# Splitting weights and activations in a fused attention, MoE and gated-MoE kernel: fewer weight operations per block, and every low part of the two MoE layers subtracted on VectorE

## The chip, the cores and the metric

One core of one Trainium2 chip runs the whole kernel. The metric is the device time of one execution in microseconds. Before the change the median of three runs is 702.15 us (702.01 to 702.81).

## The reference, cut to what matters

Three layers in float32, one behind the other: attention with pairs of queries averaged, a feed-forward layer with ELU, and a gated layer behind an RMS norm.

```
attn: q_pool = q.reshape(B, H, S//2, 2, D).mean(axis=3)        # 2, 8, 1152, 64
      softmax(q_pool @ k.T / sqrt(D)) @ v                      -> x: 1152 x 512
moe:  h = x @ w_in ; g = where(h > 0, h, exp(min(h, 0)) - 1)   # w_in 512 x 2048
      x = g @ w_out                                            # 2048 x 512
moe2: xn = x / sqrt(mean(x*x) + 1e-6) * rms_g
      (silu(xn @ w_gate) * (xn @ w_val)) @ w_out               # 512 x 1536, 1536 x 512
```

## The kernel before, in words

All activations lie transposed: 128 features on the partitions, 1152 tokens in three column blocks c of 384 tokens. TensorE multiplies a product in three passes: each operand a is split into a high part (a rounded copy, made on ScalarE) and a low part (a minus its high part), and `product` (L162) issues high by high (L167), high weight by low activation (L168) and low weight by high activation (L169) for each of four slices of 128 features. So a **product** is 12 matmuls of 128 by 384 into one of eight PSUM banks, which `bank` (L535) hands out in turn.

The order of the work on each engine is the order in which the program is written; every engine works through its own list in that order, and waits there for others.

**The weights** come as 64-bit numbers and are made into float32 by a generator, `Stream.work` (L97), 68 blocks of 128 x 512 in the order of use (in this text W0 to W67). One call of `next` on it, one *weight operation*, emits one of nine steps: the absolute value on ScalarE (L113), the low word on VectorE (L115), then the tail of the block before it, which is a step that allocates its two buffers, the high part on ScalarE (L141) and the low part (L143), and then four more steps on VectorE (L120, L122, L124, L128). `ws.step(i, k)` (L148) advances it by k, unless it is eight blocks ahead of block i. `ws.get(i)` hands out a block. Three blocks, W0 to W2, are made during the attention.

**The first MoE layer** runs in two halves of 1024 hidden features (loop L590). In each half, eight blocks i of 128 hidden features are computed for three column blocks c: one product, then `elu` (L180): ScalarE takes relu and exp (L183, L184), VectorE combines them with the bank (L187), and one product later, in `flush`, ScalarE makes the high part `gh` (L188) and GpSimd the low part `gl`. Around it stand two `ws.step(wi, 2)`. Then `out1` (L602) multiplies back: for each block m of 128 output features a quad q of four blocks, for three c. In the second half the sum is added on VectorE (L607) and squared on ScalarE (L561); GpSimd adds the squares of m = 1 and 2 (L563), VectorE those of m = 3.

The last two m of the second half are written the other way round, **the column loop** (L621): for each c, the four products n = 0 to 3 (m = 2 and 3, two quads each). Behind n = 1 of column block c, `norms[c - 1].sums` sums the squares on TensorE (L568) and takes the root (L571) and reciprocal (L572); behind n = 2, `norms[c - 1].scale` spreads it with transposes (L578) and, for four m, rescales x on VectorE (L581), makes `xh` on ScalarE (L583) and `xl`, in turn on GpSimd (even m) and on VectorE (odd m). The sums and the rescaling of the third column block stand behind the first products of the second MoE layer.

**The second MoE layer**: `unit(i, c)` (L645) is two products (gate W(32 + 2i), value W(33 + 2i)), `swiglu` (L636) takes silu on ScalarE (L638), multiplies on VectorE (L641), and one unit later makes `uh` and `ul`. The units (0, 0) and (0, 1) are multiplied first; then stands the rescaling of the third column block; then the two `swiglu` of these units, and then the units (1, 0), (1, 1), (0, 2), (1, 2) and so on.

Low parts go through two helpers: `lo_pool` (L62, recorded as line L63) on GpSimd and `lo_dve` (L68, line L69) on VectorE.

Of the kernel before, what the change touches and what calls it, by code (L numbers as in the profile page):

```python
# [38 lines left out]
def tile_kernel(ctx: ExitStack, tc: tile.TileContext, qd, kd, vd, w1d, w2d, wgd, wvd, wod, rgd, outd):  # L39
# [33 lines left out]
    class Stream:  # L73
# [60 lines left out]
        def split(self, i, w):  # L134
            self.at, self.alloc = i, True
            yield
            self.alloc = False
            pool, n = self.pools[i % WB >= NE]
            h, l = (pool.tile([128, 4, 128], F32R, tag=f"w{a}", name=f"w{a}", bufs=n) for a in "hl")
            h2, l2 = (a.rearrange("p k c -> p (k c)") for a in (h, l))  # L140
            T.copy(h2, w)  # L141
            yield
            lo_pool(l2, w, h2)  # L143
            self.parts[i] = (h, l)
            self.done += 1
            yield
# [30 lines left out]
        while pending:  # L177
            pending.pop(0)()

    def elu(ps, gh, gl, lo):  # L180

        e = hp.tile([128, CH], F32, tag="e", name="e", bufs=4)
        T.activation(out=e, in_=ps, func=AF.Relu, scale=-1.0)  # L183
        T.activation(out=e, in_=e, func=AF.Exp, scale=-1.0)  # L184
        flush()
        ws.step(wi, 2)
        V.scalar_tensor_tensor(out=e, in0=e, scalar=-1.0, in1=ps, op0=ALU.add, op1=ALU.max)  # L187
        pending.append(lambda: (T.copy(gh, e), lo(gl, e, gh)))  # L188
        ws.step(wi, 2)

    w_in = [w1d[i] for i in range(16)]
    w_out = [w2d[i] for i in range(16)]
# [326 lines left out]
    early(1)  # L519
    early(2)  # L520
    for n in range(NE):
        elu(fb[:, n, 0:CH], ge[0][:, n, :], ge[1][:, n, :], lo_pool)
    actx.close()


# [24 lines left out]
    class Norm:  # L550
# [5 lines left out]
        def square(self, m):  # L556
            c = self.c
            if m == 0:
                self.s = cp.tile([128, CH], F32, tag="sq", name="sq", bufs=3)
            q = self.s if m == 0 else hp.tile([128, CH], F32, tag="e", name="sqm", bufs=4)  # L560
            T.activation(out=q, in_=x2[:, m, cs(c)], func=AF.Square)  # L561
            if m:
                (V if m == 3 else G).tensor_tensor(out=self.s, in0=self.s, in1=q, op=ALU.add)  # L563

        def sums(self):
            b = bank()
# [7 lines left out]
        def scale(self):  # L574
            b = bank()
            c = self.c
            for n in range(3):
                PE.transpose(b[:, 128 * n:128 * n + 128], self.r[:, n:n + 1].to_broadcast([128, 128]), ident)  # L578
            for m in range(4):
                x = x2[:, m, cs(c)]  # L580
                V.scalar_tensor_tensor(out=x, in0=x, scalar=rg[:, m:m + 1], in1=b, op0=ALU.mult, op1=ALU.mult)  # L581
                h, l = xh[:, m, cs(c)], xl[:, m, cs(c)]
                T.copy(h, x)  # L583
                (lo_dve if m % 2 else lo_pool)(l, x, h)

    norms = [Norm(c) for c in range(3)]

# [2 lines left out]
    for hf in range(2):  # L590
        for i in range(8):
            w = ws.get(wi)
            for c in range(3):
                if hf == 0 and c == 0 and i < NE:
                    continue
                ps = bank()
                product(ps, w, xchunk(c), True, True)
                elu(ps, gh[:, i, cs(c)], gl[:, i, cs(c)], lo_dve if c == 1 and hf else lo_pool)
            wi += 1
        flush()  # L600

        def out1(c, m, q, b, w):  # L602
            product(b, w, g_quad(hf, q, c), q == 0, q == 1)
            if q == 1:
                x = x2[:, m, cs(c)]
                if hf:
                    V.tensor_tensor(out=x, in0=b, in1=x, op=ALU.add)  # L607
                    norms[c].square(m)
                else:
                    T.copy(x, b)  # L610

        for m in range(2 if hf else 4):
            bs = [bank() for c in range(3)]
            for q in range(2):
                for c in range(3):
                    out1(c, m, q, bs[c], ws.get(wi + q))
                    ws.step(wi + q, 4)
            wi += 2
        if hf:
            T.activation(out=dummy, in_=eps, func=AF.Sqrt)  # L620
            for c in range(3):  # L621
                for n in range(4):
                    m, q = 2 + n // 2, n % 2
                    if q == 0:
                        b = bank()
                    out1(c, m, q, b, ws.get(wi + n))
                    if c < 2 or n < 2:
                        ws.step(wi + (n if c == 2 else 0), 3)
                    if c and n == 1:
                        norms[c - 1].sums()  # L630
                    if c and n == 2:
                        norms[c - 1].scale()
            wi += 4


    def swiglu(i, c, pg, pv):  # L636
        s = hp.tile([128, CH], F32, tag="e", name="sl", bufs=4)
        T.activation(out=s, in_=pg, func=AF.Silu)  # L638
        flush()
        ws.step(wi + 2 * i if i > 1 else wi, 4)  # L640
        V.tensor_tensor(out=s, in0=pv, in1=s, op=ALU.mult)  # L641
        h, l = uh[:, i, cs(c)], ul[:, i, cs(c)]
        pending.append(lambda: (T.copy(h, s), (lo_dve if c == 1 else lo_pool)(l, s, h)))

    def unit(i, c, between=None):  # L645
        b = bank(), bank()
# [90 lines left out]
```

## Time and profile before

| | |
|---|---|
| median of three runs | 702.15 us |
| the profiled execution's own time | 702.12 us |
| its span in the profile | 700.3 us |
| TensorE matmul busy | 681.4 us (97%) |
| VectorE busy | 543.8 us (78%) |
| ScalarE busy | 416.0 us (59%) |
| GpSimd busy | 377.6 us (54%) |
| low parts of weights on GpSimd | 68 of 1467 ns |
| low parts of ELU's result on GpSimd | 37 of 1214 ns, and 3 of 1018 ns |
| low parts of the gated product on GpSimd | 24 of 1090 ns |

The attention takes the first 262 us or so, the first half of the first MoE layer lasts to about 365 us, the second to about 476 us, and the second MoE layer to the end. Time is read on TensorE: where it is idle or at a lower clock, the kernel loses time; where another engine is idle, it loses none by that alone. The page's engine rows give averages over these stages, so the table above doesn't tell which engine is late where.

### The profile page before, as it was taken

Reading aid. Unit: us, or ns where it says so; the run is one execution under the profiler, and the core shown is the slowest. Engines: PE = TensorE matmul, PEld = TensorE weight load, DVE = VectorE, ACT = ScalarE, POOL = GpSimd, SP = SyncE. Lnnn points to the kernel's source line nnn. Section 1 sums busy time; section 2 is a strip of 40 time slices with the busy share of each in tenths; the row PEclk is TensorE's granted clock in tenths of the full one; section 3 lists DMA queues with packets and bytes.
Section 4 is the critical chain, followed back from the end, with each engine's and each line's share of the span. In section 5 each row is a group of like instructions: output and inputs, shape, how many; then the busy total and the mean of one; then the engine's idle time right before and its main releaser. Section 6 shows DMA issues by size and latency. Waiting matters only on the chain.

```text
span 700.3 us, 11344 instructions
## 1 busy us (share of the span) xinstructions
PE 681.4 (97%) x4243; PEld 668.9 (96%) x4243; DVE 543.8 (78%) x891; ACT 416.0 (59%) x855; POOL 377.6 (54%) x332
## 2 busy tenths in 40 slices
PE   7999999999999999997999999999999999999998
PEld 6999999989898999986999999999999999999997
DVE  6888889898989967999978999756999876585000
ACT  5888889889887957675447774434454444342000
POOL 5988789887988305665434545442454443342000
PEclk9999999999999999997999999999999999999999
DMA  5423323433432001223432222200323222222000
GB/s 181 141 85 123 115 87 101 146 116 110 142 102 65 1 31 43 80 90 99 147 129 78 66 87 91 90 1 31 121 91 107 104 91 91 90 95 91 35 35 34
DMA packets 21607, 62.34 MB, mean 89 GB/s; under 512 B 2736, under 2 KB 4784, under 8 KB 21552
## 3 DMA queue, kind: packets, MB, share of 16 engines
q1 hardware_dynamic: 21552, 61.62, 26.6%
q8 instruction: 33, 0.54, 0.3%
q14 instruction: 22, 0.18, 0.1%
HBM read 59.25 MB, written 2.36 MB: 88 GB/s over the span
## 4 chain that ended last, share of the span: by engine, by line
PE 82%; DVE 11%; ACT 3%; POOL 1%; issue 1%; DVEq 0%; ACTq 0%; POOLq 0%
PE b L167 17%; PE b L168 17%; PE b L169 17%; PE s L279 10%; PE o L323 9%; PE t L297 8%; DVE p L283 2%; DVE ptl L69 2%; DVE wt L124 2%; DVE wt L122 2%; DVE wt L120 1%; DVE e L187 1%; POOL wl L63 1%; DVE wt L128 1%; POOL gl L63 1%
## 5 line engine op out<-in xcount | busy, mean ns | idle before, releaser
L167 PE MATMUL b<-xh,wh 128*128 128x384 f32 x468 | 157.4, 336 | 0.5 <-ACT sl L638 0.5
L169 PE MATMUL b<-xh,wl 128*128 128x384 f32 x468 | 157.1, 336 | 0.0
L168 PE MATMUL b<-xl,wh 128*128 128x384 f32 x468 | 157.0, 335 | 0.0
L63 POOL TENSOR_TENSOR wl<-wt,wh 128x512 fp32r<-128x512 f32 x68 | 99.7, 1467 | 73.9 <-ACT wh L141 57.0
L283 DVE TENSOR_SCALAR_CACHE_REDUCE p<-s 128x1152 f32<-128x1152 f32 x72 | 97.3, 1352 | 21.1 <-PE s L279 20.2
L69 DVE TENSOR_TENSOR ptl<-t,pth 128x384 fp32r<-128x384 f32 x216 | 106.6, 548 | 2.7 <-ACT pth L305 2.1
L279 PE MATMUL s<-kd,qt 128*128 128x384 f32 x480 | 97.7, 341 | 6.5 <-DVE p L283 5.0
L305 ACT CAST pth<-t 128x384 fp32r<-128x384 f32 x216 | 89.2, 487 | 23.3 <-PE t L297 22.7
L288 ACT ACTIVATE p<-p,st 128x1152 f32<-128x1152 f32 x72 | 91.3, 1268 | 6.5 <-DVE p L283 6.2
L279 PEld LDWEIGHTS s<-kd,qt 128*128 128x128 f32 x480 | 81.3, 188 | 9.7 <-DVE p L283 3.4
L167 PEld LDWEIGHTS b<-xh,wh 128*128 128x128 f32 x468 | 87.9, 188 | 1.1 <-ACT sl L638 0.9
L168 PEld LDWEIGHTS b<-xl,wh 128*128 128x128 f32 x468 | 88.0, 188 | 0.0
L169 PEld LDWEIGHTS b<-xh,wl 128*128 128x128 f32 x468 | 87.9, 188 | 0.0
L297 PE MATMUL t<-ident,p 128*128 128x128 f32 x648 | 85.7, 275 | 0.0
L113 ACT ACTIVATE wt<-wr 128x512 f32<-128x512 f32 x68 | 46.0, 676 | 66.3 <-POOL wl L63 50.3
L323 PE MATMUL o<-pth,vd 128*128 128x256 f32 (+1 forms) x288 | 84.4, 315 | 0.0
L124 DVE SCALAR_TENSOR_TENSOR wt<-wr,wt 128x512 uint32<-128x512 uint32 x68 | 80.2, 1179 | 1.8
L297 PEld LDWEIGHTS t<-ident,p 128*128 128x128 f32 x648 | 73.9, 141 | 6.6 <-DVE ptl L69 4.3
L323 PE MATMUL o<-ptl,vd 128*128 128x256 f32 (+1 forms) x288 | 78.5, 295 | 0.0
L63 POOL TENSOR_TENSOR gl<-e,gh 128x384 fp32r<-128x384 f32 x37 | 44.9, 1214 | 45.7 <-ACT gh L188 45.7
L167 PE MATMUL b<-gh,wh 128*128 128x384 f32 x180 | 62.4, 346 | 5.2 <-ACT gh L188 4.6
L128 DVE CUSTOM_DVE_ANT_0 wt<-wt,we 128x1024 uint16<-128x1024 uint16 x68 | 65.8, 968 | 1.9
(113 smaller groups left out, 1320.5 us busy)
## 6 DMA issues: line engine op xcount, KB each, us to landing
wr<-in_w_dram SPq DMA_DIRECT2D x32, 512.0 KB, 3.2
rawk<-in_k_dram SPq DMA_DIRECT2D x32, 288.0 KB, 2.9
rawq<-in_q_dram SPq DMA_DIRECT2D x15, 576.0 KB, 4.0
wr<-in_wg_dram SPq DMA_DIRECT2D x12, 512.0 KB, 3.2
wr<-in_wv_dram SPq DMA_DIRECT2D x12, 512.0 KB, 3.2
wr<-in_wo_dram SPq DMA_DIRECT2D x12, 512.0 KB, 3.2
rawv<-in_v_dram SPq DMA_DIRECT2D x16, 288.0 KB, 2.8
out_dram<-o SPq DMA_DIRECT2D x12, 192.0 KB, 1.8
```

The costliest lines, as they stand in the source:

```text
L63: G.tensor_tensor(out=o, in0=i, in1=f(h), op=ALU.subtract)
L69: V.tensor_tensor(out=o, in0=i, in1=f(h), op=ALU.subtract)
L124: V.scalar_tensor_tensor(out=t, in0=hi, scalar=0x80000000, in1=t, op0=ALU.bitwise_and, op1=ALU.bitwise_xor)
L167: PE.matmul(out, lhsT=wh[:, k, :], rhs=ah, start=first and k == 0, stop=False)
L168: PE.matmul(out, lhsT=wh[:, k, :], rhs=al, start=False, stop=False)
L169: PE.matmul(out, lhsT=wl[:, k, :], rhs=ah, start=False, stop=last and k == 3)
L279: PE.matmul(s[:, m, 0:384], lhsT=a, rhs=b[:, 384 * m:384 * m + 384], start=n == 0, stop=n == len(parts) - 1)
L283: V.tensor_scalar(out=pt, in0=s[:, :, 0:384], scalar1=-0.0625, scalar2=None, op0=ALU.mult, op1=ALU.min, accum_out=st[p][:, 0, TILES[i][4], :])
L288: T.activation(out=pt, in_=pt, func=AF.Exp, scale=-1.0, bias=st[p][:, 0, TILES[i][4], :], accum_out=st[p][:, 1, TILES[i][4], :])
L297: PE.transpose(ps[:, k, :], src[:, 128 * b:128 * b + 128], ident)
L305: T.copy(oh, re(ps))
L323: PE.matmul(self.o[:, 0:self.N], lhsT=v[:, b, :], rhs=(pth, ptl)[u][:, g["buf"], b, g["c0"]:320], start=self.n == 0, stop=self.n == 17)
```

## The change

Five places put low parts on VectorE that were on GpSimd: the weights', ELU's, the gated product's, and the norm's (`xl` of even m); the two sums of squares that GpSimd added go there too. So GpSimd has nothing to do behind the attention. The weight operations around each ELU go from 2 + 2 to 1 + 2 in the first half (nine for a block's three column blocks) and to 1 + 1 in the second (six).

```diff
@@ split
-            lo_pool(l2, w, h2)
+            lo_dve(l2, w, h2)
@@ elu
-    def elu(ps, gh, gl, lo):
+    def elu(ps, gh, gl, k=2):
...
         flush()
-        ws.step(wi, 2)
+        ws.step(wi, 1)
         V.scalar_tensor_tensor(out=e, in0=e, scalar=-1.0, in1=ps, op0=ALU.add, op1=ALU.max)
-        pending.append(lambda: (T.copy(gh, e), lo(gl, e, gh)))
-        ws.step(wi, 2)
+        pending.append(lambda: (T.copy(gh, e), lo_dve(gl, e, gh)))
+        ws.step(wi, k)
@@ the three products before the loop
-        elu(fb[:, n, 0:CH], ge[0][:, n, :], ge[1][:, n, :], lo_pool)
+        elu(fb[:, n, 0:CH], ge[0][:, n, :], ge[1][:, n, :])
@@ Norm.square
-                (V if m == 3 else G).tensor_tensor(out=self.s, in0=self.s, in1=q, op=ALU.add)
+                V.tensor_tensor(out=self.s, in0=self.s, in1=q, op=ALU.add)
@@ Norm.scale
-                (lo_dve if m % 2 else lo_pool)(l, x, h)
+                lo_dve(l, x, h)
@@ the first MoE layer
-                elu(ps, gh[:, i, cs(c)], gl[:, i, cs(c)], lo_dve if c == 1 and hf else lo_pool)
+                elu(ps, gh[:, i, cs(c)], gl[:, i, cs(c)], 2 - hf)
@@ swiglu
-        pending.append(lambda: (T.copy(h, s), (lo_dve if c == 1 else lo_pool)(l, s, h)))
+        pending.append(lambda: (T.copy(h, s), lo_dve(l, s, h)))
```

TensorE's list is the same before and after but for the buffers that it names. Three places on the other engines follow (the numbers behind names are buffers).

VectorE in the first half, in the middle of the blocks (L187 combines ELU, `wt`, `we` and `wr` are a weight being made); before:

```order
L187 SCALAR_TENSOR_TENSOR e_3569<-e_3569,b_3556 128x384
L115 TENSOR_SCALAR we_3579<-wr_3310 128x512
L187 SCALAR_TENSOR_TENSOR e_3596<-e_3596,b_3583 128x384
L120 TENSOR_SCALAR wt_3580<-wt_3580 128x512
L122 TENSOR_SCALAR wt_3580<-wt_3580 128x512
L124 SCALAR_TENSOR_TENSOR wt_3580<-wr_3310,wt_3580 128x512
L187 SCALAR_TENSOR_TENSOR e_3620<-e_3620,b_3607 128x384
L128 ISA wt_3580<-wt_3580,we_3579 128x1024
```

The same place now, one round of three ELUs:

```order
L187 SCALAR_TENSOR_TENSOR e_3592<-e_3592,b_3579 128x384
L115 TENSOR_SCALAR we_3597<-wr_3310 128x512
L69 TENSOR_TENSOR gl_3530<-e_3592,gh_3529 128x384
L187 SCALAR_TENSOR_TENSOR e_3615<-e_3615,b_3602 128x384
L69 TENSOR_TENSOR wl_3621<-wt_3496,wh_3620 128x512
L120 TENSOR_SCALAR wt_3598<-wt_3598 128x512
L69 TENSOR_TENSOR gl_3530<-e_3615,gh_3529 128x384
L122 TENSOR_SCALAR wt_3598<-wt_3598 128x512
L187 SCALAR_TENSOR_TENSOR e_3639<-e_3639,b_3626 128x384
L124 SCALAR_TENSOR_TENSOR wt_3598<-wr_3310,wt_3598 128x512
L128 ISA wt_3598<-wt_3598,we_3597 128x1024
L69 TENSOR_TENSOR gl_3530<-e_3639,gh_3529 128x384
```

Three `gl` and one `wl` have come in for every three ELUs, and there is one weight for three ELUs where there were four for nine.

VectorE in the column loop, about the first rescaling (L607 adds to x, L563 adds a square, L572 is the reciprocal, L581 rescales); before:

```order
L607 TENSOR_TENSOR x2_3525<-b_5362,x2_3525 128x384
L563 TENSOR_TENSOR sq_5161<-sq_5161,sqm_5392 128x384
L607 TENSOR_TENSOR x2_3525<-b_5395,x2_3525 128x384
L572 RECIPROCAL rr_5428<-rr_5428 128x3
L581 SCALAR_TENSOR_TENSOR x2_3525<-x2_3525,rg_61,b_5444 128x384 x2
L69 TENSOR_TENSOR xl_69<-x2_3525,xh_68 128x384
...
L607 TENSOR_TENSOR x2_3525<-b_5431,x2_3525 128x384
L563 TENSOR_TENSOR sq_5182<-sq_5182,sqm_5473 128x384
```

Now:

```order
L607 TENSOR_TENSOR x2_3525<-b_5349,x2_3525 128x384
L563 TENSOR_TENSOR sq_5119<-sq_5119,sqm_5379 128x384
L69 TENSOR_TENSOR wl_5383<-wt_5307,wh_5382 128x512
L120 TENSOR_SCALAR wt_5363<-wt_5363 128x512
L572 RECIPROCAL rr_5391<-rr_5391 128x3
L122 TENSOR_SCALAR wt_5363<-wt_5363 128x512
L124 SCALAR_TENSOR_TENSOR wt_5363<-wr_5287,wt_5363 128x512
L128 ISA wt_5363<-wt_5363,we_5362 128x1024
L581 SCALAR_TENSOR_TENSOR x2_3525<-x2_3525,rg_61,b_5412 128x384
L69 TENSOR_TENSOR xl_69<-x2_3525,xh_68 128x384
L581 SCALAR_TENSOR_TENSOR x2_3525<-x2_3525,rg_61,b_5412 128x384
```

A weight's operations stand between the square, the reciprocal and the rescaling, and each rescaling is followed by its own `xl`.

ScalarE at the third rescaling, where the second MoE layer begins (L583 makes `xh`, L638 is silu, L113 and L141 are a weight's); before:

```order
L583 CAST xh_68<-x2_3525 128x384 x4
L638 ACTIVATE sl_5646<-b_5563 128x384
L113 ACTIVATE wt_5654<-wr_5359 128x512
L638 ACTIVATE sl_5658<-b_5589 128x384
L643 CAST uh_5644<-sl_5646 128x384
L141 CAST wh_5662<-wt_5376 128x512
```

Now:

```order
L583 CAST xh_68<-x2_3525 128x384 x4
L638 ACTIVATE sl_5623<-b_5540 128x384
L113 ACTIVATE wt_5626<-wr_5409 128x512
L141 CAST wh_5629<-wt_5445 128x512
L638 ACTIVATE sl_5634<-b_5566 128x384
L643 CAST uh_5621<-sl_5623 128x384
```

And TensorE now, in unit (1, 0): the end of its first product and the start of its second:

```order
L168 MATMUL b_5648<-xl_69,wh_5461 128x384
L169 MATMUL b_5648<-xh_68,wl_5462 128x384
L167 MATMUL b_5649<-xh_68,wh_5629 128x384
L168 MATMUL b_5649<-xl_69,wh_5629 128x384
L169 MATMUL b_5649<-xh_68,wl_5630 128x384
```

The second product of unit (1, 0) reads W35, whose high part `wh_5629` now stands on ScalarE behind the four `xh` of the third rescaling; before, that product read `wh_5336`, which stood ahead of the first rescaling.

## Rows read from the trace of the kernel before

**Rows 1.** The page's first part: busy time, share of the span and instructions of TensorE (matmuls, weight loads) and the other engines.

```profile
PE 681.4 (97%) x4243; PEld 668.9 (96%) x4243; DVE 543.8 (78%) x891; ACT 416.0 (59%) x855; POOL 377.6 (54%) x332
```

**Rows 2.** What TensorE waited for in the MoE layers: us in total, times, longest.

```profile
PE b L167 <- ACT gh L188: 4.6, 1, 4.6
PE b L168 <- POOL gl L63: 1.1, 1, 1.1
PE b L568 <- DVE sq L563: 0.8, 1, 0.8
PE b L167 <- DVE e L187: 0.6, 1, 0.6
PE b L167 <- ACT sl L638: 0.5, 1, 0.5
```

**Rows 3.** Stretches of the span: start:end, length, busy time (and instructions) of PE, PEld, DVE, ACT, POOL, then TensorE's granted clock as a share of 2.4 GHz, the DMA share and GB/s.

```profile
316.00:317.00 1.00, 0.00 (x0) 0.00 (x0) 1.00 (x4) 0.27 (x1) 0.00 (x0) 0.87 0.95 311
...
326.00:328.00 2.00, 2.00 (x11) 2.00 (x10) 1.97 (x3) 0.37 (x1) 0.81 (x1) 0.75 0.00 0
```

**Rows 4.** TensorE in order of time, about the wait in the first half: start, duration, engine, line, operation, tiles, shapes, and in brackets the idle time before it and what ended it. A matmul starts before the one ahead of it has ended.

```profile
314.23 0.33 PE L169 MATMUL b<-gh,wl 128*128 128x384 f32 x1
319.16 0.69 PE L167 MATMUL b<-gh,wh 128*128 128x384 f32 x1 [4.59 <-ACT gh L188]
```

**Rows 5.** The chain that ended last, in the stretch behind that wait: start, share of the chain, what. Between the first two rows shown lie 15 more of 0.32 us.

```profile
321.60 0.32 PE b L169
...
326.72 0.32 PE b L167
327.04 0.22 PE b L168
327.26 0.18 PE b L169
```

**Rows 6.** VectorE in order of time in the first half (columns as in rows 4). From the first to the last row shown lie nine ELUs (L187) and four weights.

```profile
282.70 1.03 DVE L124 SCALAR_TENSOR_TENSOR wt<-wr,wt 128x512 uint32<-128x512 uint32 x1
...
305.49 1.40 DVE L122 TENSOR_SCALAR wt<-wt 128x512 uint32<-128x512 uint32 x1
...
307.27 1.05 DVE L124 SCALAR_TENSOR_TENSOR wt<-wr,wt 128x512 uint32<-128x512 uint32 x1
```

**Rows 7.** GpSimd in order of time, the subtraction beside that L122.

```profile
305.13 1.48 POOL L63 TENSOR_TENSOR wl<-wt,wh 128x512 fp32r<-128x512 f32 x1
```

**Rows 8.** VectorE in order of time in the second MoE layer, where GpSimd was idle beside these.

```profile
606.16 0.43 DVE L122 TENSOR_SCALAR wt<-wt 128x512 uint32<-128x512 uint32 x1
606.62 0.69 DVE L124 SCALAR_TENSOR_TENSOR wt<-wr,wt 128x512 uint32<-128x512 uint32 x1
607.69 0.56 DVE L69 TENSOR_TENSOR ul<-sl,uh 128x384 fp32r<-128x384 f32 x1 [0.38 <-ACT uh L643]
608.16 0.68 DVE L128 CUSTOM_DVE_ANT_0 wt<-wt,we 128x1024 uint16<-128x1024 uint16 x1
608.77 0.42 DVE L115 TENSOR_SCALAR we<-wr 128x512 f32<-128x512 uint32 x1
609.10 0.55 DVE L641 TENSOR_TENSOR sl<-b,sl 128x384 f32<-128x384 f32 x1
```

**Rows 9.** VectorE in order of time during the attention: the reduction of the scores (L283) behind the place where W0's low part now stands, the step L120 of a weight beside a GpSimd subtraction, and the same step by itself.

```profile
172.38 1.34 DVE L283 TENSOR_SCALAR_CACHE_REDUCE p<-s 128x1152 f32<-128x1152 f32 x1
...
175.05 1.51 DVE L120 TENSOR_SCALAR wt<-wt 128x512 f32<-128x512 f32 x1
...
206.66 0.41 DVE L120 TENSOR_SCALAR wt<-wt 128x512 f32<-128x512 f32 x1
```

**Rows 10.** VectorE in order of time about the rescalings (an L581 row of x2 is two of them).

```profile
453.89 0.56 DVE L607 TENSOR_TENSOR x<-b,x 128x384 f32<-128x384 f32 x1 [2.29 <-PE b L169]
...
456.97 1.14 DVE L581 SCALAR_TENSOR_TENSOR x<-x,rg,b 128x384 f32<-128x384 f32 x2 [1.61 <-PE b L578]
...
462.14 0.54 DVE L607 TENSOR_TENSOR x<-b,x 128x384 f32<-128x384 f32 x1
463.35 0.56 DVE L563 TENSOR_TENSOR sq<-sq,sqm 128x384 f32<-128x384 f32 x1 [0.66 <-ACT sqm L561]
...
478.78 1.14 DVE L581 SCALAR_TENSOR_TENSOR x<-x,rg,b 128x384 f32<-128x384 f32 x2 [2.04 <-PE b L578]
480.51 0.95 DVE L69 TENSOR_TENSOR xl<-x,xh 128x384 fp32r<-128x384 f32 x1 [0.58 <-ACT xh L583]
```

**Rows 11.** ScalarE in order of time behind the third rescaling: two `xh`, a silu, and the two ScalarE steps of a weight.

```profile
479.43 1.04 ACT L583 CAST xh<-x 128x384 fp32r<-128x384 f32 x2 [1.39 <-DVE x L581]
...
482.96 0.48 ACT L638 ACTIVATE sl<-b 128x384 f32<-128x384 f32 x1
483.34 0.66 ACT L113 ACTIVATE wt<-wr 128x512 f32<-128x512 f32 x1
...
486.79 0.61 ACT L141 CAST wh<-wt 128x512 fp32r<-128x512 f32 x1
```

**Rows 12.** TensorE in order of time about the norm: the sums of the second column block, the transposes of the third, and the first product of unit (1, 1).

```profile
463.96 0.83 PE L568 MATMUL b<-ones,sq 128*128 128x1 f32 x6 [0.76 <-DVE sq L563]
...
478.26 0.49 PE L578 MATMUL b<-ident,rr 128*128 128x128 f32 x3
...
483.49 0.45 PE L167 MATMUL b<-xh,wh 128*128 128x384 f32 x1 [0.55 <-ACT sl L638]
```

## The prediction

> **What bounds the kernel now.** I read the page's engine rows first: TensorE is busy 97% of the span [rows 1], so there are at most some 19 us to win, and the question is where TensorE stands still. The list of its waits names few places in the MoE layers [rows 2]: 4.6 us for ELU's high part and 1.1 us for its low part behind it, 0.6 us for VectorE, and under a microsecond each for the norm's squares and a silu. The first two are one event: at 314.23 us TensorE begins a matmul, and the next one 4.9 us later [rows 4]. While it stands, its granted clock falls from 2.4 to 1.2 GHz, and it comes back only between 326 and 328 us [rows 3]; behind the wait 17 matmuls stand 0.32 us apart, and only then 0.18 us [rows 5]. The one at 327.26 us is the 21st after the wait began. At 0.175 us each it would have begun at 314.23 + 21 x 0.175 = 317.9 us. So this event costs 9.4 us, and with the 0.6 us before it 10.0 us. That is what the change can win; nearly everything else on TensorE's path is matmuls.
>
> Its cause is VectorE. Nine ELUs and four weights take it from 282.70 to 307.27 us [rows 6], 8.19 us for three ELUs, in which TensorE needs 36 x 0.175 = 6.3 us. It is that slow because of GpSimd: L122 takes 1.40 us beside a GpSimd subtraction [rows 6, 7] and 0.43 us alone; L124 takes 0.69 us alone [rows 8].
>
> **The change in the first half.** One round is now three ELUs and one weight. From start to start, alone, a `gl` costs 0.47 us (taken from `ul`, 607.69 to 608.16), L187 the same as an instruction of its size, L128 0.61, L115 0.33, L122 0.46 [rows 8]; L124 0.69 + 0.04 and L120 0.41 + 0.04 with the step to a dependent one [rows 8, 9]. No row shows a weight's low part on VectorE. It lies between `ul` with 384 elements (0.56) and L124 with the same 512 elements and two inputs (0.69) [rows 8]; I take 0.65. Sum: 3 x 0.94 + 0.33 + 0.65 + 0.45 + 0.46 + 0.73 + 0.61 = 6.05 us. One `gl` of the round, with only L115 ahead of it, waits some 0.3 us for ScalarE: 6.05 to 6.4 us against TensorE's 6.3. VectorE no longer falls back, and the event goes: **-10.0 us**, at worst -7 if a shorter wait stays.
>
> **Attention.** Three low parts of weights now stand on VectorE, the first right ahead of the reduction at 172.38 us [rows 9], for which TensorE waits with the next scores. Beside GpSimd one costs 0.65 us to that plus 1 us (what L122 and L120 lose beside a subtraction [rows 6, 9]); three cost 2 to 5 us, of which some 0.4 us each is slack. I take **+1.8 us**, ends 0.3 and 4. What GpSimd loses there is not on the path.
>
> **The column loop.** Before, no weight operation stands between the square and the rescaling: L563, L572 and L581 follow TensorE closely. Now the stream is fewer blocks ahead, and its operations fill every product's place up to the end of the loop. The product that ended at 453.86 us (column block 1, n = 1) was not waited for long: VectorE was idle 2.29 us ahead of its L607 [rows 10]. Counting back by 2.1 us a product, those that VectorE adds up in m = 1 end at 437.1, 439.2 and 441.3, then at 445.5 and 449.7 us. Each now costs L607, 1.21 us to L563 (ScalarE's square in between, 462.14 to 463.35 [rows 10]), 0.47 us, and its share of weight steps, 1.5 to 2 us: about 3.3 us for one every 2.1 us. Adding up with the prices above, L607 starts at 437.1, 440.2, 443.6, 448.1, 451.3 and 455.1 us; then come L563 at 456.3, W33's low part, L120, and the reciprocal at about 457.8. TensorE wants to spread it at 456.4: **1.5 us**. Three more steps of the weight (1.8 us) stand ahead of the first L581, which starts at 459.7 instead of 456.97 [rows 10].
>
> The rescaling gets longer too. One m is L581 to ScalarE's `xh` 0.65 us (478.78 to 479.43), 0.52 us for it, 0.04 us to `xl` and 0.47 us to the next L581 [rows 8, 10, 11]: 1.68 us, four 6.7 us, against 5.17 us before (456.97 to 462.14 [rows 10]). So the next L607 starts at 466.4, its square is in at 468.1, and TensorE, which wants to sum at 464.7, waits **3.4 us**; before it waited 0.76 [rows 12]. Again a weight (2.5 us), an L607 and an L563 stand ahead of the second reciprocal, ready at 473.2; TensorE is there at 471.0: **2.3 us**. The third sum waits 0.2 us. In all 7.4 us against 0.8: **+6.6 us**, ends +3 and +8.
>
> **The third rescaling.** The second product of unit (1, 0) needs W35. Its high part is now on ScalarE behind the four `xh`, a silu and L113. From the end of TensorE's transposes (478.75 us before [rows 12]) the fourth `xh` ends 3 x 1.68 + 0.65 + 0.52 = 6.2 us later, the silu, L113 and L141 take 0.4, 0.57 and 0.6 us from start to start [rows 11], and the low part another 0.7. TensorE comes after one product, 2.1 us; its low-part matmul can start 8.5 us after the transposes. Two matmuls fit in between: a wait of **6.0 us**, where now 0.55 us for a silu is lost [rows 12]: **+5.5 us**, ends 4.5 and 6.5. All this counts from TensorE's own transposes, so lateness before does not hide it.
>
> **The clock.** A wait of 4.6 us brought TensorE to 1.2 GHz, for 17 matmuls at 0.32 us afterwards: 2.5 us lost, 2.8 with those at the edges [rows 2, 5]. The wait of 6.0 us should do the same: +2.8, ends 1.7 and 3.3. For the waits of 3.4 and 2.3 us the nearest rows are that event and the 0.76 us after which no half-speed matmul shows [rows 2, 12]; part of a slow stretch there would lie under the next wait: +1.2, ends 0 and 2.7.
>
> **Hidden.** In the second half with six operations a block, VectorE has 3 x 0.94 + 2.1 = 5 us of work for 6.3 us of TensorE; in the second MoE layer about 10.5 us for 12.5. There I cost the change at nothing; if a round there passed TensorE's time, products would wait for banks. The end of the kernel has neither GpSimd nor VectorE on its path.
>
> **Sum.** -10.0 + 1.8 + 6.6 + 5.5 + 4.0 = +7.9. The profiled execution took 702.12 us for its span of 700.3, the median is 702.15, so the two are one number here: **710.0 us**. With all low ends -10.0 + 0.3 + 3 + 4.5 + 1.7 = -0.5, with the high ones -7 + 4 + 8 + 6.5 + 6 = +17.5.
>
> **Rivals.** *The stream is ahead* (6%, faster). If W35 and the weights of the column loop were made before it, as they are now, no weight step would stand there; only the longer rescaling stays (+1.5 us) and attention's 1.8: 702.1 - 10.0 + 3.3 = 695.4 us. It decides whether W35's high part runs before the first rescaling. For it: stretches of spare VectorE time in the second half. Against: the program's order puts it behind the third.
>
> *Waits that cancel* (14%, about 701 to 703). VectorE comes to the first rescaling in time, because the additions of m = 1 take less than 3.3 us each. Then the loop costs +1.4, no clock falls there, and W35 stays: 702.1 - 10.0 + 1.8 + 1.4 + 5.5 + 1.7 = 702.5. It decides below some 2.3 us a product. Against: the 1.21 us to the square is a row [rows 10].
>
> *VectorE saturated* (6%, slower still). The first half's rounds stay above 6.7 us, as VectorE gets three `gl` and a `wl` more; seven rounds then use up the 3 us that TensorE's three products of the first quad leave, and the event stays: 720 us. Against: the same steps alone [rows 8]. The Trainium skill, Perfetto Trace Analysis, Optimizing Scalar/DVE Operations, has the rule for this: a saturated DVE is to be relieved, even towards GPSIMD, though the two share a port and it might not help. By that rule this change goes the wrong way; the trace bears out its second half, since L122's 1.40 and 0.43 us differ by GpSimd alone [rows 6 to 8].
>
> **How the numbers follow.** My own case has 74%, nearly all of it slower. A difference of 0.2%, 1.4 us, is about what a measurement of this kernel can tell. Faster by more: 6% for the first rival, 3% of the second, 1% of mine: 0.10. Within it: 9% of the second and 2% of mine: 0.11. Slower: 0.79. The range holds mine down to its low ends, most of the second rival and the high ends: 701 to 717.
>
> **What would show it.** Right: no wait for `gh` and no 1.2 GHz about 315 us; L122 at 0.43 us in the first half; one wait of about 6 us in TensorE's list for W35's high part on ScalarE (L141) near 480 us, with 1.2 GHz behind it; waits of 1 to 4 us for L563 and L572 before that. Wrong: a wait for `gh` near 315 us again (third rival), no wait for L141 (first), or waits of the norm that stay below 1 us each (second).

## The result, and the profile after

The changed kernel takes **705.82 us** (median of five runs, 705.04 to 707.64) where the kernel before took 702.14 beside it (701.79 to 702.81): ratio 1.0057, interval 1.0041 to 1.0073. It is slower by 3.7 us. The forecast was 710.0 us, in a range of 701 to 717: the direction is right, the size half of what was said. The profiled execution took 705.82 us, its span is 704.0.

The page's first part, and then the list of TensorE's waits (us in total, times, longest), of after:

```profile
PE 683.4 (97%) x4243; PEld 671.0 (95%) x4243; DVE 530.3 (75%) x1035; ACT 417.1 (59%) x855; POOL 194.6 (28%) x188
```

```profile
PE b L167 <- ACT wh L141: 5.6, 1, 5.6
PE b L568 <- DVE sq L563: 3.3, 1, 3.3
...
PE b L578 <- DVE rr L572: 1.2, 1, 1.2
```

The waits for `gh` and `gl` [rows 2] are gone, and three others have come: for the squares, for a reciprocal and for W35's high part. VectorE has 144 instructions more than before [rows 1] and 13.5 us less work. Where the time went is read from the same places of the program in both traces. TensorE in order of time, first of before, then of after (an L568 row is the program's three sums, six instructions in the trace; an L578 row is the three transposes):

```profile
261.77 0.34 PE L167 MATMUL b<-xh,wh 128*128 128x384 f32 x1
...
453.69 0.72 PE L568 MATMUL b<-ones,sq 128*128 128x1 f32 x6
456.44 0.49 PE L578 MATMUL b<-ident,rr 128*128 128x128 f32 x3
466.82 0.49 PE L578 MATMUL b<-ident,rr 128*128 128x128 f32 x3
475.51 0.72 PE L568 MATMUL b<-ones,sq 128*128 128x1 f32 x6
```

```profile
261.42 0.33 PE L167 MATMUL b<-xh,wh 128*128 128x384 f32 x1
...
443.14 0.72 PE L568 MATMUL b<-ones,sq 128*128 128x1 f32 x6
447.31 0.54 PE L578 MATMUL b<-ident,rr 128*128 128x128 f32 x3 [1.25 <-DVE rr L572]
457.42 1.44 PE L568 MATMUL b<-ones,sq 128*128 128x1 f32 x6 [3.30 <-DVE sq L563]
462.70 0.84 PE L578 MATMUL b<-ident,rr 128*128 128x128 f32 x3
472.01 0.83 PE L568 MATMUL b<-ones,sq 128*128 128x1 f32 x6
474.86 0.49 PE L578 MATMUL b<-ident,rr 128*128 128x128 f32 x3
483.05 0.69 PE L167 MATMUL b<-xh,wh 128*128 128x384 f32 x1 [5.58 <-ACT wh L141]
...
483.85 0.60 PE L169 MATMUL b<-xh,wl 128*128 128x384 f32 x1
...
487.39 0.33 PE L168 MATMUL b<-xl,wh 128*128 128x384 f32 x1
```

With the two rows of before that stand ahead of the prediction [rows 12]:

| place on TensorE | before | after | after less before | so this stage cost | forecast |
|---|---|---|---|---|---|
| first product behind the attention | 261.77 | 261.42 | -0.35 | attention -0.35 | +1.8 |
| first sums of squares | 453.69 | 443.14 | -10.55 | both halves -10.2 | -10.0 |
| first transposes | 456.44 | 447.31 | -9.13 | +1.4 | +1.5 |
| second sums | 463.96 | 457.42 | -6.54 | +2.6 | +3.4 less 0.76 |
| second transposes | 466.82 | 462.70 | -4.12 | +2.4 | +2.3 and +1.2 of clock |
| third sums, third transposes | 475.51, 478.26 | 472.01, 474.86 | -3.50, -3.40 | +0.7 | +0.2 |
| end | | | +3.7 | W35 and the clock +7.1 | +8.3 |

The granted clock says where TensorE works at half speed. Stretches of after (columns as in rows 3):

```profile
314.00:340.00 26.00, 26.00 (x151) 26.00 (x150) 20.31 (x39) 10.41 (x20) 0.00 (x0) 1.00 0.41 140
...
458.00:459.00 1.00, 1.00 (x6) 1.00 (x6) 1.00 (x3) 0.00 (x0) 0.00 (x0) 0.50 0.00 0
...
484.00:485.00 1.00, 1.00 (x5) 1.00 (x5) 0.96 (x3) 0.82 (x2) 0.00 (x0) 0.50 0.03 8
```

About 315 us the clock stays at 2.4 GHz. Behind the wait for the squares, and again behind that for W35, it is at 1.2. At the second transposes no wait is shown: TensorE at half speed arrives so late (462.70) that the reciprocal, done at 462.39, is there. Behind W35, 13 matmuls take 4.34 us (483.05 to 487.39) in place of 2.28, 2.1 us more. VectorE of after, in the attention, in one round of the first half, and in the first rescaling:

```profile
173.07 0.81 DVE L69 TENSOR_TENSOR wl<-wt,wh 128x512 fp32r<-128x512 f32 x1
...
176.48 0.82 DVE L120 TENSOR_SCALAR wt<-wt 128x512 f32<-128x512 f32 x1
...
283.43 0.42 DVE L122 TENSOR_SCALAR wt<-wt 128x512 uint32<-128x512 uint32 x1
...
289.51 0.42 DVE L122 TENSOR_SCALAR wt<-wt 128x512 uint32<-128x512 uint32 x1
...
449.00 0.61 DVE L581 SCALAR_TENSOR_TENSOR x<-x,rg,b 128x384 f32<-128x384 f32 x1
450.19 0.56 DVE L69 TENSOR_TENSOR xl<-x,xh 128x384 fp32r<-128x384 f32 x1 [0.58 <-ACT xh L583]
...
455.66 0.55 DVE L607 TENSOR_TENSOR x<-b,x 128x384 f32<-128x384 f32 x1
```

A round is 6.08 us (forecast 6.05 to 6.4), L122 is at 0.42; a rescaling is 6.66 us (forecast 6.7), with 0.58 us of standing for each `xh`.

### The profile page after: what moved, and what is told of

Its sections match the earlier page's. It is cut to its first block, busy times and chain, and to the rows that moved or that the text cites. A ratio compares the mean times of both kernels' runs of the same rounds, so it can differ in the third digit from the quotient of the medians.

```text
span 704.0 us, 11233 instructions
## 1 busy us (share of the span) xinstructions
PE 683.4 (97%) x4243; PEld 671.0 (95%) x4243; DVE 530.3 (75%) x1035; ACT 417.1 (59%) x855; POOL 194.6 (28%) x188
## 4 chain that ended last, share of the span: by engine, by line
PE 87%; DVE 8%; ACT 3%; DMA 1%; issue 1%; SPq 0%; ACTq 0%
PE b L167 18%; PE b L169 18%; PE b L168 18%; PE s L279 11%; PE o L323 10%; PE t L297 9%; DVE p L283 2%; DVE ptl L69 1%; DVE x L581 1%; DMA rawk<-in_k_dram 1%; DVE xl L69 1%; ACT xh L583 1%; DVE wl L69 1%; DVE wt L124 1%; DVE x L607 1%; ACT sqm L561 1%
## 5 line engine op out<-in xcount | busy, mean ns | idle before, releaser
L283 DVE TENSOR_SCALAR_CACHE_REDUCE p<-s 128x1152 f32<-128x1152 f32 x72 | 97.4, 1353 | 21.0 <-PE s L279 20.7
L169 PE MATMUL b<-gh,wl 128*128 128x384 f32 x180 | 61.2, 340 | 0.0
L168 PE MATMUL b<-gl,wh 128*128 128x384 f32 x180 | 61.2, 340 | 0.0
L69 DVE TENSOR_TENSOR wl<-wt,wh 128x512 fp32r<-128x512 f32 x68 | 47.1, 692 | 18.4 <-ACT wh L141 18.3
L113 ACT ACTIVATE wt<-wr 128x512 f32<-128x512 f32 x68 | 45.7, 672 | 25.2 <-DMA wr<-in_w_dram 10.0
L141 ACT CAST wh<-wt 128x512 fp32r<-128x512 f32 x68 | 42.1, 619 | 28.8 <-DVE wt L128 23.7
```

The source lines that it names most:

```text
L69: V.tensor_tensor(out=o, in0=i, in1=f(h), op=ALU.subtract)
L113: T.activation(out=f(t), in_=f(hi), func=AF.Abs, scale=0.125)
L168: PE.matmul(out, lhsT=wh[:, k, :], rhs=al, start=False, stop=False)
L169: PE.matmul(out, lhsT=wl[:, k, :], rhs=ah, start=False, stop=last and k == 3)
L283: V.tensor_scalar(out=pt, in0=s[:, :, 0:384], scalar1=-0.0625, scalar2=None, op0=ALU.mult, op1=ALU.min, accum_out=st[p][:, 0, TILES[i][4], :])
```

## The experiments

The kernel before was run beside every one of them and took 702.03 to 702.16 us, so their times can be compared with each other.

**Which half of the change takes the event away?** Two kernels. The first is the kernel before with the new counts alone:

```diff
-        ws.step(wi, 2)
+        ws.step(wi, 1)
...
-        ws.step(wi, 2)
+        ws.step(wi, k)
```

Here k is 2, and 1 in the blocks of the second half.

> The kernel before with the new numbers of weight operations (nine, and six in the second half) and all low parts left where they were, most of them on GpSimd. Question: which half of the change takes away the event at 314 us? If it is the number of operations: three ELUs and one weight in place of 4/3 take VectorE 8.19 less a third of a weight (1.2 us), 7.0 us, for 6.3 of TensorE; over seven rounds it falls back 5 us instead of 13, which the 8 us of slack that 13 - 4.9 leaves take in: no wait for gh, 10.2 us gained by the gl of the loop. If it is GpSimd's collisions: L122 is still 1.40 us, and a wait for gh or gl over 1 us stays there. For the rest: the column loop is late by the weight operations but its rescaling is 5.17 us, so its waits are smaller (sum under 3 us), and the wait for W35 is about 5 us with half clock behind it. Time by the first reading about 702.1 - 10.2 + 2 + 6.5 = 700 us, by the second 703 to 708 us.

Measured: 702.70 us, ratio 1.0015 (1.0006 to 1.0024). TensorE's waits in the MoE layers, and VectorE's L122:

```profile
PE b L167 <- ACT wh L141: 3.7, 1, 3.7
PE b L568 <- DVE sq L563: 2.5, 1, 2.5
...
PE b L578 <- DVE rr L572: 0.7, 1, 0.7
```

```profile
276.01 1.40 DVE L122 TENSOR_SCALAR wt<-wt 128x512 uint32<-128x512 uint32 x1
...
282.68 1.41 DVE L122 TENSOR_SCALAR wt<-wt 128x512 uint32<-128x512 uint32 x1
```

No wait for `gh` or `gl`, although GpSimd still makes L122 three times as long. A round takes 6.68 us. The counts alone win what the whole change wins there. The 700 us forecast was 2.7 too low: the loop and its clock cost 5.4 us in the profile where I allowed 2. The rescaling takes 5.16 us there, as before the change, and the second column block's squares are waited for all the same: three steps of a weight stand ahead of the first L581 (445.40 to 448.38).

The second kernel is the changed one with the counts put back to 2 + 2, so only the low parts have moved.

> The changed kernel with the old numbers of weight operations (twelve per inner block in both halves) and all low parts on VectorE. If GpSimd's collisions made the event at 314 us: three ELUs and 4/3 weights take VectorE 2.8 + 4.3 = 7.1 us alone, it falls back 0.8 us a round, 6 us in all, inside the slack of 8: no wait for gh. If twelve operations alone are too many, a wait for gh of 1 us or more stays about 314 us, or one near the end of the second half. W35 is made well ahead, so its wait is gone; four weights stand in the additions of m = 1 in place of six, so the column loop's waits are smaller than 3.3 and 1.25 us, but its rescaling is still 6.7 us. Time by the first reading 694 to 698 us, by the second above 700 us.

Measured: 702.36 us, ratio 1.0005 (0.9992 to 1.0018), 12 runs spread from 700.52 to 705.58. The profiled one took 704.94, the second longest. Its waits in the MoE layers, and a stretch (columns as in rows 3):

```profile
PE b L568 <- DVE sq L563: 3.0, 3, 2.2
PE b L167 <- ACT gh L188: 2.5, 1, 2.5
PE b L167 <- ACT sl L638: 2.4, 1, 2.4
...
315.00:320.00 5.00, 4.74 (x14) 4.34 (x15) 4.72 (x10) 3.28 (x8) 0.00 (x0) 0.50 0.32 108
```

A wait for `gh` stays, at 315 us, with the clock at 0.50 of full speed from 315 to 320: the second reading. No trace shows how much of this wait the shorter runs have (their mean granted clock goes up to 0.998, the profiled one's is 0.990); none of the 12 comes near the first reading's 694 to 698 us. The wait for W35 is gone, as expected, and one for a silu stands there. From 281.32 to 303.56 VectorE passes four weights and nine ELUs, 7.4 us a round. So the rounds rank 8.19 (before), 7.4 (low parts alone), 6.68 (counts alone), 6.08 (both), for TensorE's 6.3; down to 6.68 the slack suffices.

**The wait for W35.** The changed kernel with one line more ahead of the third rescaling:

```diff
+    ws.get(wi + 3)
     norms[2].scale()
```

> The changed kernel with the operations of W34 and W35 written ahead of the third rescaling, nothing else moved. My theory: TensorE's wait for W35's high part (5.58 us, 483.05) and the half clock behind it go; they make the 7.1 us between the third transposes (3.4 us ahead of the kernel before) and the end (3.7 us behind it). The third rescaling starts some 2 us later, which nothing waits for, since its chunk is read six products further on. Time about 705.8 - 7.1 = 698.7 us, with the waits of the column loop (3.3 and 1.25 us) still there. Rival A: the weight only pushes the same lateness into the rescaling, and TensorE waits for xh or xl of chunk 2, or for W35 all the same: 703 us or more. Rival B: the half clock stays because the chip pulls TensorE back there for another reason than the wait: about 701.5 us.

Measured: 702.58 us, ratio 1.0009 (1.0001 to 1.0018): a gain of 3.2, not 7.1. W35's wait is gone and another stands in its place. TensorE, then ScalarE:

```profile
482.49 0.69 PE L167 MATMUL b<-xh,wh 128*128 128x384 f32 x1 [3.39 <-ACT sl L638]
```

```profile
479.88 0.51 ACT L583 CAST xh<-x 128x384 fp32r<-128x384 f32 x1 [1.15 <-DVE x L581]
481.54 0.51 ACT L583 CAST xh<-x 128x384 fp32r<-128x384 f32 x1 [1.15 <-DVE x L581]
481.96 0.48 ACT L638 ACTIVATE sl<-b 128x384 f32<-128x384 f32 x1
```

The first silu stands on ScalarE behind four `xh` that come every 1.66 us, and TensorE needs the bank that it frees. Rival A held in kind only: the lateness stayed, but what is late is a silu, which neither reading named. Under one wait lay the next. So both are taken away, with the silus and their products written ahead of the rescaling:

```diff
+    act = []
+    for i, c, pg, pv in first:
+        s = hp.tile([128, CH], F32, tag="e", name="sl", bufs=4)
+        T.activation(out=s, in_=pg, func=AF.Silu)
+        V.tensor_tensor(out=s, in0=pv, in1=s, op=ALU.mult)
+        act.append((i, c, s))
+    ws.get(wi + 3)
     norms[2].scale()
...
```

The rest of the two `swiglu`, the weight operations and the low parts, stays behind the rescaling.

> W35's operations ahead of the third rescaling, as in the kernel with only that, and also the first two silus and their products with the other half ahead of it. There TensorE waited 3.39 us for the first silu, which stood on ScalarE behind the four xh of the rescaling and which gives the bank for the next product free, and ran nine matmuls at half speed behind that (1.3 us). My theory: that wait had been lying under the wait for W35, and with both gone no wait over 1 us is left from 474 to 490 us: 702.6 - 3.4 - 1.3 = 697.9 us. Rival: the lateness moves on once more, to the next silu or to xh of chunk 2 (VectorE's rescaling starts about 1 us later), and 701 to 703 us stay.

Measured: 697.35 us, ratio 0.9938 (0.9925 to 0.9951). The stretch about the third rescaling:

```profile
464.00:490.00 26.00, 25.87 (x152) 25.52 (x152) 18.15 (x36) 11.53 (x23) 0.00 (x0) 1.00 0.07 25
```

The stage's 7.1 us, and the 0.55 us that the kernel before lost to the silu, are all won. Some 0.5 us of the 0.8 beyond them are a shorter stretch of half speed in the loop, as far as one profile of each tells.

**The price of the clock.** The changed kernel with 32 matmuls in the wait, whose results the next product overwrites:

```diff
+            if n and (i, c) == (1, 0):
+                wd = ws.get(2 * i + wi)[0]
+                for k in range(32):
+                    PE.matmul(b[1], lhsT=wd[:, k % 4, :], rhs=xh[:, k % 4, cs(c)], start=True, stop=True)
             product(b[n], ...)
```

> The changed kernel with 32 extra matmuls (0.175 us each, 5.6 us in all) on TensorE where it waits for W35's high part; their results are overwritten by the product that follows. The wait stays, but TensorE works through it. My theory: the half clock behind the wait (13 matmuls in 4.34 us from 483.05 instead of 2.28) comes from standing still, so it goes: granted clock 1.00 from 478 to 490 us, and 705.8 - 2.1 = 703.7 us. Rival: the half clock is not caused by the wait but by something else at that place: 705.8 us, with half speed as before. Third: the extra matmuls end after W35 is there and cost their own time: 706.3 us or more.

Measured: 703.71 us, ratio 1.0027 (1.0016 to 1.0038). TensorE, then a stretch:

```profile
476.74 5.71 PE L651 MATMUL b<-xh,wh 128*128 128x384 f32 x32
482.49 0.44 PE L167 MATMUL b<-xh,wh 128*128 128x384 f32 x1
```

```profile
484.00:485.00 1.00, 1.00 (x8) 1.00 (x7) 0.93 (x3) 0.25 (x1) 0.00 (x0) 1.00 0.00 0
```

The product starts as long behind the transposes as in the changed kernel (8.19 us), but at full clock: half speed comes from standing still. Its first 14 matmuls start within 2.77 us in place of 4.34, so half speed costs 1.6 us there; the third matmul, at 483.22, now comes late, behind W35's low part (VectorE has it at 483.16), which half speed had covered. The other 0.5 us of the gain lies ahead of it: the third transposes come at 474.30 in this profile, behind a shorter stretch of half speed in the loop.

**The length of the rescaling.** The changed kernel with each `xl` written behind the next L581:

```diff
+            low = None
             for m in range(4):
...
                 T.copy(h, x)
-                lo_dve(l, x, h)
+                if low:
+                    lo_dve(*low)
+                low = (l, x, h)
+            lo_dve(*low)
```

> The changed kernel with the low part of each quarter of the rescaling written behind the next quarter's L581, so VectorE no longer stands idle 0.58 us for each xh. One rescaling takes VectorE about 4 x (0.5 + 0.47) + 0.5 = 4.4 us instead of 6.66. My theory: the length of the rescaling makes the wait for the squares (3.30 us) and 2.3 us of the wait for W35 (5.58). The first becomes about 1 us, the second about 3.4, the half clock behind the first goes or shrinks by a half; a wait of 1 to 2 us for the second reciprocal may come up instead, which half clock had covered. 699 to 701 us. Rival: the weight operations that stand on VectorE in the loop make the waits, the rescaling only shifts them: the loop's waits and half clock stay within 0.5 us, only W35's wait shrinks, about 703.3 us.

Measured: 700.60 us (699.07 to 702.76), ratio 0.9981 (0.9970 to 0.9992); the rescaling goes from 449.24 to 453.57, 4.33 us.

```profile
PE b L578 <- DVE rr L572: 3.3, 2, 2.0
PE b L167 <- ACT wh L141: 3.3, 1, 3.3
...
PE b L568 <- DVE sq L563: 1.0, 1, 1.0
```

As expected: both waits are shorter by 2.3 us, and the second reciprocal's comes up at 2.0.

**More weights in the second half.** The changed kernel with nine operations there too (`k` always 2).

> The changed kernel with nine weight operations per inner block in the second half too. Two more weights are then made when the first rescaling begins (37 in place of 35), so W35 is long there: its wait and half clock go, 7.1 us. In the additions of m = 1 and up to the second reciprocal the same number of weight operations stands on VectorE as now. My theory: the column loop's waits stay about as they are (3 and 1 us, with half clock), 705.8 - 7.1 = 698.7 us. The rival of my prediction that the stream is ahead gave 695.4 us, with no wait over 1 us in the loop. Third: nine operations are too many beside the ELUs of the second half (6.05 to 6.4 us of VectorE work for 6.3 us), and a wait appears there or at the first squares: over 700 us.

Measured: 699.48 us, ratio 0.9963 (0.9951 to 0.9975).

```profile
PE b L167 <- ACT sl L638: 2.4, 1, 2.4
PE b L578 <- DVE rr L572: 1.9, 1, 1.9
...
PE b L568 <- DVE sq L563: 0.6, 1, 0.6
```

The time is near the 698.7 of my theory, but by luck: W35's wait goes and the silu's takes its place, as above, while the wait for the second column block's squares shrinks from 3.3 to 0.6 us, which I had denied. No weight operation (the stream is at its limit, eight blocks ahead) stands between the first reciprocal and the rescaling on VectorE, which begins 0.6 us behind the transposes (448.89, 449.47) in place of 1.7 (447.31, 449.00); and TensorE, with 1.9 us of waiting and half speed behind it, comes later to the squares. This is the condition of the prediction's first rival, and it gives 699.5 us, not 695.4, because of these two waits and the silu's.

**All of it together.** Nine operations in both halves, the shorter rescaling, the silus ahead of the third one, and the additions of squares written behind the weight operations that followed them:

```diff
-            if m:
-                V.tensor_tensor(out=self.s, in0=self.s, in1=q, op=ALU.add)
+            self.q = q if m else None
...
```

The addition itself stands in a function `add`, called behind the next `ws.step`.

> All low parts on VectorE, nine operations in both halves, the rescaling with the low parts one quarter behind, the additions of squares behind the next weight operations, and the first two silus ahead of the third rescaling. With nine operations alone 699.48 us were measured, with waits of 1.92 us (second-chunk reciprocal), 0.61 (square), 2.44 (silu) and two short stretches of half clock (about 1.4 us in 450 to 455, 1.7 in 480 to 485, each half lost: some 1.5 us). If VectorE's length in the loop and ScalarE's queue behind the rescaling make these, all go: 699.5 - 4.9 - 1.5 = 693 us. If the weight operations alone make the loop late: the wait for the reciprocal stays near 2 us, with half clock: 696 us. If something new comes behind (the adds stand later, xl is later by one quarter), above 697 us.

Measured: **691.44 us** (690.93 to 691.83), ratio 0.9852 (0.9839 to 0.9865): faster than both kernels. The page, and TensorE's only waits behind the attention (L581 and L575 are now the lines of the transposes and the reciprocal):

```profile
PE 678.0 (98%) x4243; PEld 666.1 (97%) x4243; DVE 528.0 (77%) x1035; ACT 416.3 (60%) x855; POOL 194.4 (28%) x188
...
PEclk9999999999999999999999999999999999999999
```

```profile
PE b L581 <- DVE rr L575: 1.2, 2, 0.7
```

Three kernels take one thing out of it. With the additions of squares back in their place:

> The combined kernel with the additions of squares back right behind L607 (VectorE stands 0.59 us for each square). Measured with them moved: 691.44 us, TensorE's waits for the reciprocals 0.70 and 0.46 us, none for squares. If that idle time is a part of the lateness in the additions of m = 1 (six or more of them, 0.6 us each, as the step of the prediction had it with 1.21 us from L607 to L563), the waits for the reciprocals are 1.5 to 2 us, the second perhaps with half clock: 693 to 696 us. If nine operations, the rescaling and the silus were enough by themselves: 691.5 us.

693.59 us (691.71 to 694.80). One reciprocal is waited for 1.88 us, and the granted clock from 437 to 464 us is 0.94: VectorE's standing for squares was a part of the lateness. But one of its four runs, 691.71 us at a mean granted clock of 1.00, is as fast as the combined kernel, so the price of the order in time seems to hang on half speed; that was not tried. With six operations and W35 forced:

> The combined kernel with six weight operations per inner block in the second half, as in the changed kernel, and W35's operations written ahead of the first two silus. The number of weight operations between the second half and the first reciprocal is the same as with nine (six weights), so I expect the loop as in the combined kernel and no wait for W35: 691.5 to 692.5 us. Rival: the two weights less that are ready stand in VectorE's way in the loop or behind the third rescaling (waits over 1 us for a reciprocal, a silu or a weight): over 694 us.

693.04 us (692.77 to 694.06): four waits, 0.41 to 1.31 us, 3.1 in all, in place of 1.2, no half speed. I expected the loop unchanged; the order alone does not carry it, the weights made ahead help by some 1.6 us (W35's place differs as well, but the waits lie ahead of it). With most low parts back on GpSimd:

> The combined kernel with the low parts of the weights, of the ELUs (all but column block 1 of the second half) and of the products of the second MoE layer (all but column block 1) back on GpSimd, where the kernel before had them; the norm and the rescaling stay on VectorE. Question: does it matter which engine subtracts, once nothing in the program stands late? If only the order and the counts matter: 691.5 us within 1 us. If GpSimd's collisions matter (L122 1.40 us in place of 0.43): with nine operations a round of the second half takes VectorE 7 us for TensorE's 6.3, it falls back up to 5 us by its end, and the additions of m = 1 are late: waits of 2 to 4 us in the loop, 694 to 698 us.

694.32 us (693.63 to 694.65), against 691.44: so it does matter who subtracts. TensorE waits 1.65 us for a reciprocal and 1.05 for a square. In the second half, where nine operations stand beside three ELUs, L122 recurs every 6.94 us (364.22, 371.17, 378.11) where it comes every 6.24 with VectorE alone.

## Why the prediction was half right

**The event of the first half: right in size, its cause only half told.** Forecast -10.0, measured -10.2. The step "It is that slow because of GpSimd" explains the 1.40 us, but the event goes with GpSimd's collisions still there: the counts suffice; with the low parts alone the profiled run still has a wait. The size was read a little high, too: rows 5 give shares of a chain, and the 21st matmul itself starts at 327.10 us,

```profile
327.10 0.34 PE L169 MATMUL b<-gh,wl 128*128 128x384 f32 x1
```

so the event was 9.2 us and the term -9.8. On the question put there, the Trainium skill (Perfetto Trace Analysis, Optimizing Scalar/DVE Operations) says that offloading work from a saturated VectorE, even to GpSimd, may make sense, but might not help between these two, as they share a port. The rule speaks for the kernel with low parts on GpSimd; the runs bear out the second half, though none shows that the port is the reason: the whole page of before has VectorE at 543.8 us [rows 1], after at 530.3 with more to do, and the last experiment loses 2.9 us by the move back.

**Attention: the step that failed.** Forecast +1.8 (0.3 to 4), measured -0.35, below my low end. The step is "What GpSimd loses there is not on the path". I priced the three low parts that VectorE gets and forgot that it gives back what GpSimd's subtractions had cost it. Added are 0.81, 0.82 and 0.67 us, 2.3 in all. L120 falls from 1.51 [rows 9] to 0.82; two L124 and an L122, from 1.38, 1.37 and 1.37 to 0.68, 0.68 and 0.54; one L120 rises from 0.41 to 0.80: 2.5 us returned. VectorE of before, and of after:

```profile
182.86 1.38 DVE L124 SCALAR_TENSOR_TENSOR wt<-wr,wt 128x512 uint32<-128x512 uint32 x1
...
210.66 1.37 DVE L122 TENSOR_SCALAR wt<-wt 128x512 uint32<-128x512 uint32 x1
```

```profile
183.60 0.68 DVE L124 SCALAR_TENSOR_TENSOR wt<-wr,wt 128x512 uint32<-128x512 uint32 x1
...
211.43 0.54 DVE L122 TENSOR_SCALAR wt<-wt 128x512 uint32<-128x512 uint32 x1
```

Ten profiles have this attention code; the first layer's third product ends with a matmul that starts between 260.1 and 261.9 us in them, and at 261.4 to 261.6 in the three with GpSimd. So the -0.35 itself is inside the scatter: the term is about nothing.

**The column loop: mechanism right, +7.2 with its clock where I had +7.8.** The first two places in the table are within 0.1 us of the sum by prices (waits of 1.25 and 3.30 us for 1.5 and 3.4). The path came out too: shifted by the 10.55 us that TensorE is ahead, the six L607 ahead of the first rescaling start within 0.2 us of the times I had, and so do the first L581 and the next L607 (449.00 and 455.66 in the trace, so 459.6 and 466.2 for 459.7 and 466.4). Behind them I counted a wait (2.3) and a share of clock (1.2) one upon the other; half speed took the wait's place, and both together were 3.1 with the third sums.

**W35: mechanism right, +7.1 for +8.3.** The wait was 5.58 us for 6.0, with half speed 7.1 us in all for 8.3. The low-part matmul starts 8.5 us behind the transposes (475.35 to 483.85), as I had it; ahead of it two matmuls at half speed fill 0.8 us where I had put 0.35 and counted the rest as waiting. I took 2.8 us of clock from the earlier event, where 17 matmuls ran slowly; here it was 13, 2.1 us. What the prediction did not see is that taking W35 out would win only 3.2 us, since a silu's wait of 3.4 lay below.

**Rivals.** That the stream is ahead did not happen (W35 came behind the rescaling), nor that waits cancel (3.3 us in the loop), nor a saturated VectorE (rounds at 6.08). The forecast missed by 4.2 us: 2.2 of attention, 0.2 of the event, 0.6 of the loop, 1.2 of W35 and its clock.

## What to carry to other kernels

When work moves off an engine, price what its going gives back to the neighbours that collided with it, not only what it costs where it arrives. When one wait is taken away, look for what would have been late next in the same stretch: here a silu stood behind the same four copies. And before an operation that waits for another engine's answer, write one that doesn't: four subtractions moved by one place each took 2.3 us from a rescaling.

## What the runs showed that was not expected

- The low parts of two layers moved to VectorE, and VectorE's total fell by 13.5 us. Its L124 averages 700 ns after and 1179 before, L128 690 and 968, L122 428 and 793 (68 of each).
- L124 beside GpSimd took 1.66 us in the last experiment's second half, 0.69 alone, with L122 at 0.43 a step earlier (417.04 and 416.58, where the products of `out1` run; beside the ELUs L124 stays at 0.68): which instruction pays depends on where GpSimd's subtraction falls.
- How long half speed lasts differs between executions of the same code. From 437 to 464 us the granted clock is 0.87 in the profile of after and 0.94 in those of the kernels with W35 early, with the silus early and with the filled wait, which run the same program up to there; from the first to the third transposes the four take 27.55, 26.99, 27.02 and 26.98 us, so it is worth some 0.55 us. Among the runs of one kernel the longer ones show the lower mean clock: low parts alone 700.52 us at 0.997 and 705.58 at 0.988, the shorter rescaling 699.07 at 0.997 and 702.76 at 0.992, while the combined kernel's four are at 1.00 and lie within 0.9 us. But two kernels with half speed, nine operations and the filled wait, spread no more than 1.2 us. What makes half speed last longer in one execution than in the next was not tried.
